# Attention and a two-layer block on one core: one fp32 identity, value scalings shared between two engines, and new orders for all engines

## The chip, the core and the metric

The kernel runs on one core of one Trainium2 chip. TensorE (PE in the profile) multiplies matrices; VectorE (DVE), ScalarE (ACT) and GpSimd (POOL) work on tiles; SyncE (SP) issues most transfers. The metric is the device time of one execution in microseconds. Durations are those of one profiled execution; lines of the program are written L692 for line 692.

## The reference, cut to what matters

Linear attention with a decay per head, in blocks of 64 positions, and then two dense layers with a "snake" between them. Batch 4, 8 heads, 768 positions, 64 values a head; 3072 rows of 512 go through layers of 2048 and 512.

```python
for b in range(nb):
    qb, kb, vb = (q[:, :, sl], k[:, :, sl], v[:, :, sl])
    intra = np.einsum('bhic,bhjc->bhij', qb, kb) * Dmask[None]
    intra = np.einsum('bhij,bhjd->bhid', intra, vb)
    inter = np.einsum('bhid,bhde->bhie', qb * lam_pow[None], kv_state)
    out[:, :, sl] = intra + inter
    kv_state = lam_block * kv_state + np.einsum('bhsd,bhse->bhde', kb * rev_pow[None], vb)
x = out.transpose(0, 2, 1, 3).reshape(B * S, H * D)
h = x @ w_in
s = np.sin(alpha * h)
g = h + s * s / (alpha + 1e-09)
return g @ w_out
```

`Dmask` is `lam ** (i - j)` for `i >= j` and 0 above the diagonal.

## The kernel before, in words

The work is cut into 24 units and 6 groups. A unit is four heads of one batch entry over 256 positions; four units make a group of 512 rows, which then goes through both layers. Each piece of work is an operation with a name, and u is its unit, g its group, f one of 16 column blocks of 128 of the first layer, m one of four row blocks:

- `ld{u}q`, `ld{u}k`, `ld{u}v` (SP, L475) load 256 KB each; three buffers for each of q, k and v. `cq`, `ck` (L493, L495) cast q and k to bf16; `sv` (L501) multiplies v by the table `R`, the reciprocal of the decay powers.
- `tq`, `tk` (PE, L511) transpose q and k against the identity `iden`, and `e0{u}`, `e1{u}` (L518, L520) copy the result out of PSUM: `e02` is unit 2's q, `e12` its k. From unit 9 on a transposing transfer `dt` (SP, L524) does this.
- `sc` (PE, L535) makes scores, `mm` (DVE, L543) masks them, `kv` (PE, L569) makes the products for the state, `kc` (ACT, L623, L579) copies them out, `bx`, `d0`, `d1` (L597, L611) and `n0`, `n1` (L635) multiply by decay tables on POOL or DVE, `in` and `io` (PE, L645, L658) make the output, and `oe` (DVE, L677) multiplies it by the table `ET` and writes it to `xt`. For units 8 to 23 `step{u}` holds the PE part of two units at once.
- `f1_g_f` (PE, L692) is the first layer, `sn` (ACT, L699) the sine, `sq` (ACT L706 or POOL L708) its square, `g_g_f` (DVE, L711) the sum, written to `gall`. `f1_0_0` is cut into two halves, `f1_0_0_0` and `f1_0_0_1`. `f2_g_m_j` (PE, L728) is a quarter of the second layer, four matmuls of 512 columns; `ev` (ACT, L734) copies the result out and `out` (SP, L759) sends it. The very last block, group 5 and m = 3, is cut by columns into 256, 128 and 128 (`f2_5_3_ja`, `b`, `c`) with `end0` to `end2` and `send0` to `send2`.
- `wi0` to `wi3` and `wo0` to `wo3` are the loads of the weights, issued by POOL (L457, L462): `wi0` brings columns 0 to 255 of `w_in`, `wi1` 256 to 767, `wi2` 768 to 1279, `wi3` the rest.
- `warm` (PE, L768) is filler, a matmul of ones of 512 or 256 columns.

At the start, two small inputs are loaded by ACT. `lamb` (PE, L405) spreads `lam` over the partitions, `tabc` (DVE, L408) copies it, `tab1` (POOL, L411) raises it to the powers of the position, `tabm` (DVE, L415) and `tab2` (DVE, L418) make the tables `E` and `R`, `tabi` (POOL, L422) makes two 64x64 identities in `id2`, `tabd` (POOL, L426 and L428) multiplies them by `E`, `tab0` (PE, L434) turns that into the evictions' table, `tab4` and `tab3` copy it to `LBD` and `ET`. `alpha` (PE, L446) transposes alpha against an identity `idf`, and `alphav` (DVE) copies it and takes its reciprocal.

What each engine does, in which order, is written out by hand in the table `SEQ` (L173): five lists of names. An engine takes its list from the front, strictly in order. A planner (`Plan.run`, L47) replays the lists with a cost per operation, only to settle in which order the program's instructions are written and which of several buffers each takes. PSUM has four banks `f` (first layer, second layer, transposes, early kv products, filler), one for scores (`s`) and a pair for outputs (`okv`); operations give a bank back when its last reader is done. The output buffers `ob` are three.

Of the kernel before, what the change touches and what calls it, by code (L numbers as in the profile page):

```python
# [12 lines left out]
FP32 = mybir.dt.float32  # L13
# [16 lines left out]
class Plan:  # L30
# [6 lines left out]
    HOLD, SHARE = 1.5, 0.35  # L37

# [8 lines left out]
    def run(self, seq):  # L47
# [28 lines left out]
        while len(order) < len(self.ops):  # L76
# [28 lines left out]
            for e in self.ENG:  # L105
# [9 lines left out]
                if e == "PE" and op.mode is not None:  # L115
                    c += self.SWITCH * (op.mode != mode)
                    mode = op.mode
                op.start, op.eng = t, e
# [3 lines left out]
                free[e] = t + c  # L122
# [23 lines left out]
def kernel(  # L146
# [28 lines left out]
            "warm warm warm warm lamb warm warm warm warm warm warm warm warm warm warm warm tq0 "  # L175
            "warm alpha tk0 warm warm warm tq1 warm tab0 kv0 sc0 tk1 warm tq2 warm warm warm sc1 "
# [29 lines left out]
        "DVE":  # L206
# [17 lines left out]
        "ACT":  # L224
# [65 lines left out]
    NXT = 3  # L290
    WI = (256, 512, 512, 768)
    WO = (4, 4, 4, 4)
    HALVES = ()
    NWARM = 9
    NLAM = 2
    DMAT = {9, 10, 11, 12, 13, 14, 15, 16, 17, 18, 19, 20, 21, 22, 23}
# [782 lines left out]
```

## Time and profile before

| | |
|---|---|
| time, median of 3 runs | 215.76 us (215.47 to 215.77) |
| the profiled execution | 215.8 us, its span 214.0 us |
| granted TensorE clock over the span | 1.000 |
| DVE busy | 119.7 us, 56% of the span |
| ACT busy | 138.9 us, 65% |
| POOL busy | 131.4 us, 61% |
| chain that ended last: PE's share | 91% |
| bytes moved | 33.65 MB, mean 157 GB/s |

The span runs from the first to the last instruction; the device time is 1.8 us longer in this execution. Busy shares are means over stages that differ: PE fills with filler and small products at the start and with large matmuls later, POOL has its work in the first 140 us, and DVE and ACT are thin in the last 50 us.

```profile
PE   8988999999999999999999999999999999999993
DVE  2387775557388774676968868865546224212101
ACT  3573788555699667878888789466578746336021
POOL 7998899297899699898988998530351030002100
DMA  5999999989899999899977744031240022031544
```

These are tenths of busy time in 40 slices of 5.35 us each.

### The profile page before, as it was taken

Reading aid. Unit: us, or ns where it says so; the run is one execution under the profiler, and the core shown is the slowest. Engines: PE = TensorE matmul, PEld = TensorE weight load, DVE = VectorE, ACT = ScalarE, POOL = GpSimd, SP = SyncE. Lnnn points to the kernel's source line nnn. Section 1 sums busy time; section 2 is a strip of 40 time slices with the busy share of each in tenths; the row PEclk is TensorE's granted clock in tenths of the full one; section 3 lists DMA queues with packets and bytes.
Section 4 is the critical chain, followed back from the end, with each engine's and each line's share of the span. In section 5 each row is a group of like instructions: output and inputs, shape, how many; then the busy total and the mean of one; then the engine's idle time right before and its main releaser. Section 6 shows DMA issues by size and latency. Waiting matters only on the chain.

```text
span 214.0 us, 5247 instructions
## 1 busy us (share of the span) xinstructions
PE 205.2 (96%) x2053; PEld 106.5 (50%) x2082; DVE 119.7 (56%) x175; ACT 138.9 (65%) x251; POOL 131.4 (61%) x212
## 2 busy tenths in 40 slices
PE   8988999999999999999999999999999999999993
PEld 3656444455445555555555555554444444444543
DVE  2387775557388774676968868865546224212101
ACT  3573788555699667878888789466578746336021
POOL 7998899297899699898988998530351030002100
PEclk9999999999999999999999999999999999999999
DMA  5999999989899999899977744031240022031544
GB/s 162 303 284 205 204 162 173 283 233 287 248 247 294 229 200 253 265 241 216 293 177 188 164 91 84 3 72 29 49 98 2 0 52 49 0 73 42 135 91 107
DMA packets 62347, 33.65 MB, mean 157 GB/s; under 512 B 18018, under 2 KB 59378, under 8 KB 62322
## 3 DMA queue, kind: packets, MB, share of 16 engines
q1 hardware_dynamic: 57824, 28.91, 57.4%
q0 software_dynamic: 4224, 4.19, 12.5%
q8 instruction: 16, 0.26, 0.5%
q10 hardware_dynamic: 274, 0.21, 0.3%
q14 instruction: 9, 0.07, 0.1%
HBM read 27.27 MB, written 6.29 MB: 157 GB/s over the span
## 4 chain that ended last, share of the span: by engine, by line
PE 91%; DVE 2%; ACT 2%; POOL 2%; issue 1%
PE hps L692 38%; PE ops L728 36%; PE sp L535 3%; PE okv L728 3%; PE okv L658 3%; PE bz L768 3%; PE okv L645 2%; PE pt L511 1%; DVE gall L711 1%; PE okv L569 1%; POOL vb L501 1%; ACT s L699 1%; ACT s L706 1%; DVE sm L543 1%; PE kp L569 0%
## 5 line engine op out<-in xcount | busy, mean ns | idle before, releaser
L711 DVE SCALAR_TENSOR_TENSOR gall<-s,r_sb,hps 128x512 bf16<-128x512 bf16 (+1 forms) x97 | 69.6, 739 | 59.7 <-ACT s L706 42.6
L692 PE MATMUL hps<-xt,w_in_sb 128*128 128x512 bf16 (+1 forms) x367 | 90.3, 377 | 1.7 <-DVE gall L711 0.4
L699 ACT ACTIVATE s<-hps,alpha_sb 128x512 bf16<-128x512 f32 (+1 forms) x97 | 65.5, 680 | 28.5 <-PE hps L692 27.4
L728 PE MATMUL ops<-w_out_sb,gall 128*128 128x512 bf16 (+2 forms) x378 | 82.1, 361 | 0.6 <-issue 0.5
L708 POOL TENSOR_TENSOR s<-s 128x512 bf16<-128x512 bf16 x31 | 32.2, 1042 | 48.6 <-ACT s L699 46.5
L728 PEld LDWEIGHTS <-gall 128*128 128x128 bf16 x416 | 38.8, 98 | 41.9 <-DVE gall L711 0.2
L692 PEld LDWEIGHTS <-w_in_sb 128*128 128x128 bf16 x388 | 36.4, 98 | 42.0 <-issue 1.7
L706 ACT ACTIVATE s<-s 128x512 bf16<-128x512 bf16 (+1 forms) x66 | 40.3, 621 | 1.2
L543 DVE TENSOR_TENSOR sm<-sp,mask 128x1024 bf16<-128x1024 f32 x24 | 29.2, 1218 | 1.2 <-PE sp L535 1.2
L501 POOL TENSOR_TENSOR vb<-st_v,R 128x512 bf16<-128x512 f32 x24 | 25.0, 1044 | 1.4 <-DMA st_v<-in_v_dram 0.9
L734 ACT COPY ob<-ops 128x512 f32<-128x512 f32 x21 | 12.2, 585 | 18.8 <-PE ops L728 18.8
L597 POOL TENSOR_TENSOR kvbd<-kvx,LBD 128x256 bf16<-128x256 f32 x32 | 19.7, 614 | 2.5
L677 DVE TENSOR_TENSOR xt<-okv,ET 128x512 bf16<-128x512 f32 x24 | 16.5, 687 | 6.2 <-ACT kva L579 3.9
L594 POOL TENSOR_TENSOR kvx<-kva,kvs 128x128 f32<-128x128 f32 x32 | 14.6, 456 | 6.9 <-ACT kva L579 6.7
L495 POOL CAST qk<-st_k 128x512 bf16<-128x512 f32 x18 | 10.9, 614 | 4.1 <-DMA st_k<-in_k_dram 4.1
L535 PE MATMUL sp<-qt 64*64 64x128 bf16 x384 | 10.2, 221 | 0.8 <-issue 0.4
L493 ACT CAST qk<-st_q 128x512 bf16<-128x512 f32 x13 | 8.0, 622 | 3.8 <-DMA st_q<-in_q_dram 3.8
L658 PE MATMUL okv<-sm,vb 64*64 64x128 bf16 x384 | 9.7, 218 | 0.5 <-DVE sm L543 0.5
L768 PE MATMUL bz<-const-bfloat16-1.0 128*128 128x256 bf16 (+1 forms) x33 | 9.2, 395 | 0.8 <-PEq L1063 0.8
L518 ACT COPY qt<-pt 128x512 bf16<-128x512 bf16 x11 | 6.4, 591 | 5.2 <-PE pt L511 5.2
L579 ACT COPY kva<-okv 128x256 f32<-128x256 f32 (+1 forms) x16 | 5.1, 316 | 6.9 <-PE okv L569 6.8
L635 POOL TENSOR_TENSOR kvs<-kvx,ET 128x128 f32<-128x128 f32 x24 | 9.4, 403 | 0.0
(63 smaller groups left out, 109.9 us busy)
## 6 DMA issues: line engine op xcount, KB each, us to landing
st_q<-in_q_dram SPq DMA_DIRECT2D x24, 256.0 KB, 4.6
st_k<-in_k_dram SPq DMA_DIRECT2D x23, 256.0 KB, 4.3
out_dram<-ob SPq DMA_DIRECT2D x45, 128.0 KB, 2.4
st_v<-in_v_dram SPq DMA_DIRECT2D x22, 256.0 KB, 4.5
w_out_sb<-in_moe_w_out_dram POOLq DMA_DIRECT2D x4, 512.0 KB, 8.7
w_in_sb<-in_moe_w_in_dram POOLq DMA_DIRECT2D x2, 512.0 KB, 7.3
w_in_sb<-in_moe_w_in_dram POOLq DMA_DIRECT2D x1, 768.0 KB, 10.3
st_v<-in_v_dram SPq DMA_DIRECT2D x4, 128.0 KB, 3.5
```

What stands on the lines that cost most here:

```text
L501: ENGINE[op.eng].tensor_tensor(out=T[u, "vb"][:], in0=T[u, "v"][:].rearrange("p h two e -> p two h e"), in1=R[:, :, hs].unsqueeze(3).to_br ...
L535: nc.tensor.matmul(out=T[u, "sp"][half[c], hd, par, hp, :], lhsT=QT[half[hd], 1, par, hp, half[c]], rhs=QT[half[hd], 0, :, hp, half[c]], s ...
L543: V.tensor_tensor(out=T[u, "sm"][:].rearrange("p hd par hp i -> p (hd par) hp i"), in0=T[u, "sp"][:].rearrange("p hd par hp i -> p (hd par ...
L597: G.tensor_tensor(out=bd[:], in0=X.unsqueeze(2).to_broadcast([P, 2, 2, D]), in1=LBD[:, hs, :].unsqueeze(3).to_broadcast([P, 2, 2, D]), op= ...
L658: nc.tensor.matmul(out=okv[half[hd], c, hp * P:(hp + 1) * P], lhsT=VB[half[c], par, 2 * hp + hd, :], rhs=ST[half[c], hd, par, hp, :], star ...
L677: V.tensor_tensor(out=o, in0=i, in1=ET[:, 2 * hh:2 * hh + 2].rearrange("p hp two e -> p hp (two e)") .unsqueeze(1).to_broadcast([P, 2, 2, ...
L692: op.ins = nc.tensor.matmul(out=op.tile[:, cols], lhsT=w_in_sb[:, c, f * P:(f + 1) * P], rhs=xt[g][:, c].rearrange("p b c i -> p (b c i)") ...
L699: A.activation(out=op.tile[:, cols], in_=mm.tile[:, cols], func=ACTF.Sin, scale=alpha_sb[:, f:f + 1])
L706: A.activation(out=op.tile[:, cols], in_=s1, func=ACTF.Square)
L708: ENGINE[op.eng].tensor_tensor(out=op.tile[:, cols], in0=s1, in1=s1, op=ALU.mult)
L711: V.scalar_tensor_tensor(out=gall[g][:, f, cols], in0=sq.tile[:, cols], scalar=r_sb[:, f:f + 1], in1=mm.tile[:, cols], op0=ALU.mult, op1=A ...
L728: op.ins = nc.tensor.matmul(out=first.tile[:, cols], lhsT=gall[g][:, f, m * P:(m + 1) * P], rhs=w_out_sb[:, f, cols], start=(f == 0), stop ...
```

## The change

A single fp32 identity of 128x128 is made on POOL; DVE copies from it the bf16 identity and the two 64x64 ones; `tabi` is gone, `tabd` and 14 of the 24 `sv` go to DVE, and one query cast goes from ACT to DVE. All five lists in `SEQ` are new; the number of fillers (33) stays. The planner gets two corrections to its costs and `out_5_0` another cost. Where each operation runs, counted from the lists:

| | before | after |
|---|---|---|
| `sv` | POOL 24 | POOL 10, DVE 14 (units 0, 2, 4, 6, 8, 11, 13 to 16, 19 to 22) |
| `cq`, `ck` | ACT 18, POOL 29, DVE 1 | ACT 15, POOL 32, DVE 1 |
| `e0`, `e1` | ACT 11, DVE 7 | ACT 10, DVE 8 |
| `sq` | ACT 66, POOL 31 | ACT 64, POOL 33 |
| `warm` ahead of `f1_0_0_0` | 33 | 26 |

```diff
-    iden = consts.tile([P, P], BF16, name="iden")
-    make_identity(nc, iden[:])
-    idf = consts.tile([NFC, NFC], FP32, name="idf")
-    make_identity(nc, idf[:])
+    idf = consts.tile([P, P], FP32, name="idf")
+    make_identity(nc, idf[:])
+    iden = consts.tile([P, P], BF16, name="iden")
     id2 = consts.tile([P, D], FP32, name="id2")
...
+    for c in range(2):
+        V.tensor_copy(out=id2[half[c], :], in_=idf[half[c], half[c]])
+    V.tensor_copy(out=iden[:], in_=idf[:])
...
-    def tables_i(op):
-        for c in range(2):
-            make_identity(nc, id2[half[c], :])
-
     def tables_d(op):
+        eng = ENGINE[op.eng]
         for hd in range(2):
-            G.tensor_copy(out=E2[half[hd]], in_=E[half[hd]]
+            eng.tensor_copy(out=E2[half[hd]], in_=E[half[hd]]
...
-        G.tensor_tensor(out=ED[:], in0=id2[:].unsqueeze(1).to_broadcast([P, HP * 2, D]),
+        eng.tensor_tensor(out=ED[:], in0=id2[:].unsqueeze(1).to_broadcast([P, HP * 2, D]),
...
-    SV = [("POOL", 1.05)]
+    SV = [("POOL", 1.05), ("DVE", .83)]
...
+    COLD = 6.9
+    OVER = {"PE": 0, "DVE": .08, "ACT": .09, "POOL": .04, "SP": 0}
...
+                    c *= 2 if t < self.COLD else 1
...
-                free[e] = t + c
+                free[e] = t + max(c - self.OVER[e], .02)
```

The lists, up to the first full block of the first layer and around the places that are spoken of:

```diff
 "PE":
-  warm warm warm warm lamb warm x11 tq0 warm alpha tk0 warm x3 tq1 warm tab0 kv0 sc0 tk1 warm tq2
-  warm x3 sc1 warm tk2 kv1 in0 io0 sc2 warm kv2 warm in1 tq3 io1 warm tk3 in2 io2 sc3 kv3 warm x2
-  tq4 in3 warm x3 io3 f1_0_0_0 tk4 f1_0_0_1 f1_0_1 sc4 kv4 f1_0_5 in4 f1_0_2 ...
+  warm x5 lamb warm x5 alpha tq1 tq0 warm tk0 tab0 warm x2 sc0 tk1 kv0 warm tq2 warm sc1 in0 tk2
+  warm kv2 io0 sc2 kv1 warm x6 tq3 warm tk3 in1 io1 tq4 sc3 warm kv3 warm x2 in2 io2 tk4 in3 io3
+  f1_0_0_0 kv4 sc4 f1_0_1 f1_0_0_1 f1_0_4 f1_0_5 in4 io4 f1_0_3 f1_0_2 warm f1_0_7 warm f1_0_8
+  warm f1_0_6 ... tq5 f2_0_0_3 tq6 tk5 f2_0_3_2 sc5 kv6 tk6 f2_0_3_3 kv5 sc6 warm tq7 ...
+  f1_1_9 warm warm f1_1_0 ... f2_5_3_2a f2_5_3_3a warm f2_5_3_0b ...
 "DVE":
-  tabc tabm tab2 ck0 alphav tab4 mm0 e02 mm1 oe0 mm2 oe1 e13 oe2 bx3 mm3 oe3 e14 ...
+  tabc tabm tabd cq0 tab2 e10 e00 sv0 tab4 alphav mm0 sv2 mm1 oe0 mm2 e13 oe1 mm3 bx3 oe2 e14 sv4 oe3
+  bx4 mm4 ... sv6 e15 e06 mm5 ... oe7 e08 sv8 e18 ... g_1_14 sv15 oe11 sv14 sv13 mm12 ...
 "ACT":
-  cq0 e00 cq1 e01 e10 kc0 tab3 e11 ck2 e12 kc1 cq3 kc2 ck3 e03 cq4 e04 kc3 ...
+  cq1 e01 ck1 e11 kc0 tab3 ck2 e12 e02 kc2 kc1 ck3 cq4 e03 ck4 e04 kc3 ...
 "POOL":
-  iden tab1 tabi tabd sv0 ck1 cq2 bx0 sv1 wi0 sv2 bx1 wi1 bx2 sv3 wi2 wi3 ck4 n03 ...
+  iden tab1 ck0 cq2 bx0 sv1 wi0 cq3 wi1 bx1 sv3 bx2 wi2 wi3 n02 wo0 ...
 "SP":
-  ld0k ld0q ld1q ld0v ld1k ld2q ld1v ld2k ld2v ld3q ld3v ld3k ld4q ld4k ld4v ... out_5_2 send0 out_5_1
-  out_5_0 send1 send2
+  ld1q ld0q ld0k ld1k ld0v ld2q ld2k ld2v ld1v ld3q ld4q ld3k ld3v ld4k ld4v ... out_4_1 out_5_0 send0
+  send1 send2
```

More of the change, by code (lines that the diff above doesn't have):

```diff
@@ L174 @@
         "PE":
-            "warm warm warm warm lamb warm warm warm warm warm warm warm warm warm warm warm tq0 "
-            "warm alpha tk0 warm warm warm tq1 warm tab0 kv0 sc0 tk1 warm tq2 warm warm warm sc1 "
[29 rows of a table removed]
-        "DVE":
[17 rows of a table removed]
-        "ACT":
[30 rows of a table removed]
-        "POOL":
[21 rows of a table removed]
+            "warm warm warm warm warm lamb warm warm warm warm warm alpha tq1 tq0 warm tk0 tab0 warm "
[31 rows of a table added]
+        "DVE":
[18 rows of a table added]
+        "ACT":
[28 rows of a table added]
+        "POOL":
[20 rows of a table added]
     }
     QS = set()
-    CK0 = [("ACT", .62), ("DVE", .43)]
     SPLIT = {(22, 2), (23, 1), (23, 2)}
@@ L292 @@
     WO = (4, 4, 4, 4)
-    HALVES = ()
+    HALVES = ({0}, set())
     NWARM = 9
@@ L296 @@
     DMAT = {9, 10, 11, 12, 13, 14, 15, 16, 17, 18, 19, 20, 21, 22, 23}
-    NH0 = 1
     KVF = {0, 1, 2, 3, 4, 5}
@@ L304 @@
     CK = [("ACT", .62), ("POOL", .62)]
-    SV = [("POOL", 1.05)]
-    EV0 = [('DVE', 0.41), ('ACT', 0.59)]
-    EV1 = [('DVE', 0.41), ('ACT', 0.59)]
+    SV = [("POOL", 1.05), ("DVE", .83)]
+    EVH = [("DVE", 0.42), ("ACT", 0.59)]
+    CK0 = [("ACT", .62), ("POOL", .62), ("DVE", .43)]
     dw = lambda cols: {128: .030, 256: .05, 384: .066, 512: .081, 640: .1, 768: .12, 1024: .16}[cols]
@@ L445, in alphas @@
         ap = bank(op, "f", [P, NFC], FP32, "ap")
-        nc.tensor.transpose(out=ap[:], in_=alpha_r[:], identity=idf[:])
+        nc.tensor.transpose(out=ap[:], in_=alpha_r[:], identity=idf[:NFC, :NFC])
         op.tile = ap
@@ L770, in dummy @@
                              start=True, stop=True)
-        dop = add("warm", on("PE", 0.40), [], dummy, take=("f",), mode="n")
+        dop = add("warm", on("PE", 0.2135), [], dummy, take=("f",), mode="n")
         dop.give, dop.part = ((dop, "f"),), 1
@@ L775 @@
     idq = add("iden", on("POOL", 1.85), [], lambda op: None)
-    lamd = add("lamb", on("PE", .4), [lamq, first], lam_all, take=("f",), lag=PEL, mode="n")
+    lamd = add("lamb", on("PE", .1), [lamq, first], lam_all, take=("f",), lag=PEL, mode="n")
     tbc = add("tabc", on("DVE", .12), [lamd], tables_c, give=((lamd, "f"),))
@@ L779 @@
     tbm = add("tabm", on("DVE", .17), [tb1], tables_m)
-    tbi = add("tabi", on("POOL", .95), [idq], tables_i)
-    tbd = add("tabd", on("POOL", 1.7), [tbm, tbi], tables_d)
+    tbd = add("tabd", [("POOL", 1.55), ("DVE", .95)], [tbm, idq], tables_d)
     tb2 = add("tab2", on("DVE", .25), [tbm], tables_v)
@@ L787 @@
     alq = add("alq", on("ACT", .01), [lamq], lambda op: None, lag=1.2)
-    alphas_op = add("alpha", on("PE", 0.2), [alq], alphas, take=("f",), lag=PEL, mode="n")
+    alphas_op = add("alpha", on("PE", 0.16), [alq, idq], alphas, take=("f",), lag=PEL, mode="n")
     al2 = add("alphav", on("DVE", 0.4), [alphas_op], alphas_v, give=((alphas_op, "f"),))
@@ L813, in make_unit @@
         early = u < NT
-        cq = add(f"cq{u}", CQS if u in QS else CQ if u else CK0, [lq, tbm if u in QS else None],
+        cq = add(f"cq{u}", CQS if u in QS else CK if u else CK0, [lq, tbm if u in QS else None],
                  lambda op: cast(op, u, 0), take=("qk",), give=((lq, "st0"),),
@@ L821, in make_unit @@
         if u not in DMAT:
-            tq = add(f"tq{u}", on("PE", .22), [cq], lambda op: turn_pe(op, u, 0),
+            tq = add(f"tq{u}", on("PE", .22), [cq, idq], lambda op: turn_pe(op, u, 0),
                      take=("f", "qt"), give=((cq, "qk"),), lag=PEL, mode="n")
-            e0 = add(f"e0{u}", EV0, [tq], lambda op: turn_ev(op, tq, u, 0),
+            e0 = add(f"e0{u}", EVH, [tq], lambda op: turn_ev(op, tq, u, 0),
                      give=((tq, "f"),))
@@ L827, in make_unit @@
                      take=("f",), give=((cq, "qk"),), lag=PEL, mode="n")
-            e1 = add(f"e1{u}", EV1, [tk], lambda op: turn_ev(op, tk, u, 1),
+            e1 = add(f"e1{u}", EVH, [tk], lambda op: turn_ev(op, tk, u, 1),
                      give=((tk, "f"),))
@@ L994, in make_f2 @@
                  take=("ob",), give=owe)
-        st = add(f"out_{g}_{m}", on("SP", 1.0), [ev], lambda op: f2st(op, ev, g, m),
+        st = add(f"out_{g}_{m}", on("SP", .55 if (g, m) == (NG - 1, 0) else 1.0), [ev], lambda op: f2st(op, ev, g, m),
                  give=((ev, "ob"),), dma=(.65, .08))
@@ L1017 @@
     assert at == {"i": DFF, "o": NFC}
-    for f in range(NFC):
-        for hb in ((0, 1) if f < NH0 else (None,)):
-            make_f1(0, f, hb)
-    for hb in ((0, 1) if 1 in HALVES else (None,)):
+    for g in range(2):
         for f in range(NFC):
-            make_f1(1, f, hb)
+            for hb in ((0, 1) if f in HALVES[g] else (None,)):
+                make_f1(g, f, hb)
     def gate_of(x):
```

192 rows, old and new, of the table SEQ are left out of this document.

## The prediction, made before the changed kernel was run

> **What bounds the kernel now.** I read the table by stage first. Its columns are the stretch, its length, busy time and instruction count of PE, PEld, DVE, ACT and POOL, then granted clock, DMA share and GB/s.
>
> ```profile
> 15.00:20.00 5.00, 3.69 (x101) 2.73 (x99) 3.41 (x6) 2.14 (x6) 4.28 (x8) 1.00 1.28 214
> 22.69:54.42 31.73, 31.22 (x307) 15.55 (x312) 20.46 (x29) 21.05 (x41) 25.01 (x38) 1.00 1.06 228
> 60.00:140.00 80.00, 79.03 (x1003) 42.26 (x1020) 59.24 (x78) 63.70 (x114) 69.45 (x116) 1.00 0.87 193
> 150.00:205.00 55.00, 54.74 (x260) 25.67 (x264) 17.86 (x25) 28.73 (x48) 10.37 (x10) 1.00 0.22 49
> ```
>
> Behind 22.69 us TensorE stands still for 0.5, 1.0 and 0.3 us in the three later rows, and much of that is missing matmul records: a run of n matmuls of 512 columns goes at 0.216 us each (24 in 5.18 us in the chain of waits), and where the count of a run is one short the gap is 0.22. So past 22.69 nothing but TensorE's own work sets the time, and no order can win there; it can only lose. What is not TensorE's work lies ahead of it. The timeline of PE at the start (start, duration, line, tiles, count, idle time before with what ended it):
>
> ```profile
> 0.77 1.87 PE L768 MATMUL bz<-const-bfloat16-1.0 128*128 128x512 bf16 x4 [0.77 <-PEq L1063]
> 2.56 0.59 PE L405 MATMUL lp<-lam_r,row 1*128 1x8 f32 x2
> 3.09 3.55 PE L768 MATMUL bz<-const-bfloat16-1.0 128*128 128x512 bf16 x11
> 7.30 0.49 PE L768 MATMUL bz<-const-bfloat16-1.0 128*128 128x256 bf16 x3
> 19.74 0.61 PE L692 MATMUL hps<-xt,w_in_sb 128*128 128x256 bf16 x4
> 22.69 1.02 PE L692 MATMUL hps<-xt,w_in_sb 128*128 128x512 bf16 x4 [0.18 <-DVE gall L711]
> ```
>
> L768 is filler, which costs nothing as long as TensorE would wait. All 33 fillers lie ahead of 18.9 us. At 22.69 units 0 to 3, unit 4 up to its scores and kv product, and f1_0_0_0, f1_0_0_1 and f1_0_1 are done. That point compares the two orders. Before it a chain over DVE, ACT and POOL counts, and the weights:
>
> ```profile
> 6.84 1.04 POOL L428 TENSOR_TENSOR ED<-id,E 128x512 f32<-128x512 f32 x1
> 7.84 1.04 POOL L501 TENSOR_TENSOR vb<-st_v,R 128x512 bf16<-128x512 f32 x1
> 11.79 0.95 POOL L457 DMA_DIRECT2D w_in_sb<-in_moe_w_in_dram  x1
> 14.34 0.80 POOL L457 DMA_DIRECT2D w_in_sb<-in_moe_w_in_dram  x1
> 10.08 1.23 DVE L543 TENSOR_TENSOR sm<-sp,mask 128x1024 bf16<-128x1024 f32 x1 [0.29 <-PE sp L535]
> 18.12 1.22 DVE L543 TENSOR_TENSOR sm<-sp,mask 128x1024 bf16<-128x1024 f32 x1
> w_in_sb<-in_moe_w_in_dram POOLq DMA_DIRECT2D x2, 512.0 KB, 7.3
> ```
>
> **Identities.** POOL loses the 16x16 pair (0.10 + 0.19) and L422's four instructions with their gaps (5.09 to 6.34, 1.25 us). DVE gains three copies, by its nearest row (the copy at L408, 0.17) 0.5 us, between 2.41 and 3.19 where it waits for lp. They cost nothing; without that cover, up to 0.5 on the chain.
>
> **The start, step by step** (before's time in brackets). PE now runs five fillers ahead of lamb, 0.427 each (1.87 us hold four): lamb 2.92 (2.56). With before's own distances lam_bc 3.55, the power on POOL 3.80 to 5.48, E complete 5.7. tabd on DVE: two copies at 0.17 and a product whose nearest row is the mask at L388 (0.69, two f32 inputs in SBUF; above, POOL's 1.04): done 6.75 (7.88). cq0 moves from ACT to DVE behind it, 0.36: 7.05, so tq0 at 7.1 (6.47), tk0 7.45, tab0 7.7 (8.40), sc0 8.85 (9.61). Ahead of the first mask DVE has e10 and e00 (0.41 each), sv0 (0.69 to 1.04; I take 0.69, from the row of the same engine and size), tab4 0.33, alphav 0.42: first mask 9.9 (10.08). Second, behind sv2: 11.66 (11.83). Third: sc2 waits for e02, queued on ACT behind kc0, tab3, ck2 and e12 from 10.1 (0.43, 0.60, 0.65, 0.59, then 0.59): 13.7 (13.77). Fourth: sv1's v is now the ninth load; before's ninth was issued at 6.26, and st_v takes 4.5 to 5.4, so about 11.65; then on POOL sv1 1.04, the first w_in issue 0.95, cq3 0.61, the second issue 0.80, bx1 0.61: 15.6. in1 and io1 follow at 15.85, oe1 16.3, sc3 16.45, mask 16.94 (18.12). Then bx3 0.42, oe2 to 19.1 (okv has one buffer: in3 waits for it), io3 19.35, f1_0_0_0 19.7 (19.74), kv4 and sc4 to 20.75, oe3 20.7, f1_0_1 20.75 and f1_0_0_1 (0.86 + 0.43): f1_0_4 at 22.1 with the same work done as before at 22.69. **Lead 0.59 us.** Bounds: none, if the three scalings on DVE take 1.04 and ACT's queue is as tight as worked out; and 1.1, because f1_0_4 reads columns of the second w_in transfer, which before lands at 14.34 + 7.2 = 21.6. The same 15 loads and the first w_in transfer lie ahead of it, and the DMA share is full from 5 us on, so no order of POOL brings it earlier.
>
> **Fillers.** Of the same 33 seven now stand behind 22 us: after f1_0_2, f1_0_7 and f1_0_8, one after sc6, two after f1_1_9, one ahead of the last end block. Each is 0.11 (three start within 0.22 us). Where before has no waits, a filler is lost time, and where after has one there, that wait is the loss: +0.76; bounds 0.33 (the three around units 5 to 8 hidden by those units' latency, and one more) and 0.77.
>
> **Units 5 to 7** hang on loads gated by the second w_out transfer. Seven second-layer blocks instead of eight lie between tq5 and the last io; one block of 0.86 stands ahead of tq5 instead. sv6 on DVE ahead of e15 waits for its v, now fourth in that row of loads instead of sixth. ck5 and cq5 waited for loads (4.13 and 0.89 us idle), so this chain gives nothing; I cost it 0, its cover being the seven blocks (6.0 us), and half a block, 0.4, if one wait shows.
>
> **Ten more scalings on DVE** (14 in all) in the stage of steps: 10 x 0.69 = 6.9, DVE 66.1 of 80 us busy instead of 59.2; POOL 10.4 less. Queued behind each are masks, oe and gates, for which PE's banks wait. Between two steps stand about four blocks of 0.86, which cover one scaling, or two ahead of mask 12 (1.4). I take +0.1, bounds 0 and 1.6 (0.1 a step). Three casts and two squares fewer on ACT (3 x 0.62 + 2 x 0.62 = 3.1 us) meet an engine with waits of 27 us for hps: 0.
>
> **Loads and transposes** on SP keep their number; each is moved past others, but their waits end on casts, and PE stood behind none of them: 0. The planner's COLD and OVER are no instructions.
>
> **Tail.** The last two column blocks are 0.89 apart as before. ev_5_0 ends 2.1 us ahead of the last matmul, out_5_0 goes out on SP (0.47) and ACT (0.55), and end0, on ACT behind that issue, starts 0.3 late; send0 (0.59 twice) then pushes send1 and send2 on SP, the last starting 0.58 after the last matmul instead of 0.34 (ACT's 0.39): +0.1, bounds -0.3 (out_5_0's 256 KB are out of the way) and +0.4.
>
> Sum: -0.59 + 0.76 + 0.10 + 0.10 = +0.37. The profiled execution is 215.8 (span 214.0 and 1.8 around it), the median 215.76: **216.1 us**.
>
> [...] DVE L388 ran from 1.69 to 2.38; POOL's select of a 128x128 tile began at 1.89 and took 0.65, against 0.23 to 0.24 for 64x64: it ended 0.16 after L388. [...]
>
> **Rivals.** (1) *The lead reaches the weights.* ACT's and POOL's queues run looser than worked out, f1_0_4 starts at 21.6, and the three middle fillers vanish in waits of units 5 to 8: -1.1 + 0.43 + 0.1, 215.2. For it: the fourth mask gains 1.2 us. Against: e02 and sv1 stand behind four others. It decides from f1_0_4 before 21.75.
>
> [...]
>
> (3) *The clock opens late.* Fillers of 512 columns go at 0.43 us until 5.2, 128 columns at 0.056 from 6.47: half pace, then full. After leaves PE empty from 6.0 to 7.1. At half pace tab0 takes 1.9 instead of 0.96 and the first mask comes 0.45 later: 216.5. [...]
>
> (4) *The start wins nothing*: lead 0, 216.7.
>
> **Numbers.** Within 0.2% (0.43 us) is what a measurement here cannot tell from no change. Forecast 0.45, own range 215.7 to 216.7, about half on each side of 216.19: same 0.22, slower 0.23. Rival 1 0.22: faster 0.15, same 0.07. Rival 2 0.23, rivals 3 and 4 0.05 each: slower. Together faster 0.15, same 0.29, slower 0.56; range 215.1 to 217.6.
>
> **What would show it.** lp at 2.9; first mask 9.9, fourth near 16.9; f1_0_4 near 22.1; filler rows after 22 us with no wait ahead of them; PE idle in 60 to 140 within 0.3 of before's; the last SP issue 0.6 after the last matmul. Wrong would be a start of f1_0_4 ahead of 21.5, or a wait of a us or more on PE behind sm, xt or gall.

## The result and the profile after

The changed kernel takes 221.26 us (220.62 to 222.06), the kernel before, on the same chip, 215.64 us (215.47 to 215.90): a ratio of 1.026, 95% interval 1.024 to 1.029. It is slower by 5.6 us, and far outside of the range forecast. Three kernels further down (x3_cq0act, x4_ld13v, f1_pool) had one slow execution each, more than 1.5% above their fastest; medians and ratios leave it out.

The profiled execution has a span of 219.4 us against 214.0. Three distances add up to it: f1_0_0_0 starts at 22.09 us instead of 19.74 (+2.35), from there to the last matmul it takes 193.13 us instead of 190.69 (+2.44), and from the last matmul to the end of the span 4.19 instead of 3.59 (+0.60). Here and below the last matmul is placed where its weight load ends, 0.04 to 0.05 us behind its start.

The busy tenths of the changed kernel in 40 slices of its span:

```profile
PE   8788999999999999799999999999999999999992
DVE  3688766528568974989959995986645552100001
ACT  3266788637389663797896778679657883311120
POOL 6259765499789989997867796433353001100000
DMA  6999999997999999998979756002021131242163
```

TensorE looks as full as before, but for the 7 in the second slice (5.5 to 11.0 us) and the 7 in the 17th (87.8 to 93.2 us), of which more below. A full PE row does not mean useful work: fillers, products at half pace and lost turns count as busy. Here is the table by stage (stretch, length, busy time and count of PE, PEld, DVE, ACT, POOL, then granted clock, DMA share, GB/s):

```profile
15.00:20.00 5.00, 4.42 (x136) 3.28 (x124) 4.05 (x6) 4.34 (x12) 4.98 (x8) 1.00 0.86 136
22.69:54.42 31.73, 31.15 (x312) 15.37 (x312) 19.54 (x31) 22.76 (x44) 22.83 (x38) 1.00 1.08 222
60.00:140.00 80.00, 78.36 (x960) 41.02 (x958) 65.12 (x85) 61.96 (x112) 66.95 (x107) 1.00 0.90 201
150.00:205.00 55.00, 55.00 (x275) 25.33 (x274) 18.80 (x26) 29.31 (x48) 10.17 (x10) 1.00 0.21 49
```

In the stage of steps DVE rose from 59.2 to 65.1 us, near the 66.1 worked out. POOL fell by 2.5 only, from 69.45 to 66.95, though its scalings in this stretch went from 14 to 6 (14.6 us to 6.3): two squares and two casts more came in, and a cast took 0.68 us in the mean instead of 0.61.

**The start.** The timeline of PE (start, duration, line, tiles, count, idle time before with what ended it):

```profile
0.78 2.29 PE L767 MATMUL bz<-const-bfloat16-1.0 128*128 128x512 bf16 x5 [0.78 <-PEq L1059]
3.00 0.59 PE L407 MATMUL lp<-lam_r,row 1*128 1x8 f32 x2
5.77 0.61 PE L510 MATMUL pt<-iden,qk 128*128 128x128 bf16 x4
7.64 0.61 PE L510 MATMUL pt<-iden,qk 128*128 128x128 bf16 x4 [1.27 <-DVE qk L494]
8.69 2.02 PE L433 MATMUL et<-ED,ones 128*128 128x512 f32 x2
11.06 0.64 PE L534 MATMUL sp<-qt 64*64 64x128 bf16 x16
```

lp comes at 3.00 as forecast (2.92). Then tq0 (7.64) waits for cq0 on DVE, and PE is empty for 1.27 us. The trace's record of the clock has it open at 12.73 us, where before it opened at 6.45. Until then the rows show half pace: fillers of 512 columns at 0.42 us each (five in 2.10) instead of 0.22, four transposes in 0.61 us instead of 0.40, tab0 in 2.02 instead of the 0.96 worked out. The first mask starts at 11.76 us instead of 9.9.

**The fillers behind 22 us.**

```profile
28.44 0.27 PE L767 MATMUL bz<-const-bfloat16-1.0 128*128 128x256 bf16 x1
28.77 1.02 PE L691 MATMUL hps<-xt,w_in_sb 128*128 128x512 bf16 x4
29.63 0.27 PE L767 MATMUL bz<-const-bfloat16-1.0 128*128 128x256 bf16 x1
29.96 1.02 PE L691 MATMUL hps<-xt,w_in_sb 128*128 128x512 bf16 x4
```

A block of four goes on after 0.86 us (28.77 to 29.63), but the block behind a filler starts 0.33 us after the filler did. The filler's own turn is 0.11; the other 0.22 is a wait for the filler's end. The trace has it: the block at 29.96 waits for one semaphore, the one that the filler ahead of it raises as it ends, at 29.90. That fits a block that takes over the filler's bank. The last filler, at 213.33, has a follower without such a wait, and it costs 0.11. The seven together take 1.87 us in these rows.

**Step 13.** DVE, then SP, then PE:

```profile
84.78 1.11 DVE L500 TENSOR_TENSOR vb<-st_v,R 128x512 bf16<-128x512 f32 x1
88.27 0.89 DVE L500 TENSOR_TENSOR vb<-st_v,R 128x512 bf16<-128x512 f32 x1 [2.38 <-POOL s L707]
89.08 1.21 DVE L542 TENSOR_TENSOR sm<-sp,mask 128x1024 bf16<-128x1024 f32 x1
```

```profile
81.20 2.54 SPq L758 DMA_DIRECT2D out_dram<-ob  x4
83.84 0.53 SPq L474 DMA_DIRECT2D st_v<-in_v_dram  x1
```

```profile
88.83 0.39 PE L644 MATMUL okv<-qt,kvbd 128*128 128x128 bf16 x4
90.34 0.42 PE L534 MATMUL sp<-qt 64*64 64x128 bf16 x16 [1.12 <-DVE sm L542]
```

The scaling at 88.27 is sv13. It waits 2.38 us, the mask of unit 12 stands behind it, and PE waits 1.12 us for the mask: the 7 in the row of tenths. The trace names a square on POOL as the releaser, but sv13 needs its v: ld13v stands on SP behind the four transfers of out_0_1 and out_0_2 and is issued at 83.84 only.

**The tail.** SP's last transfers, after and then before:

```profile
213.31 3.84 SPq L748 DMA_DIRECT2D out_dram<-ob  x5
```

```profile
209.50 1.92 SPq L749 DMA_DIRECT2D out_dram<-ob  x3
```

Five transfers in a row instead of three; the last issue starts 1.22 us behind the last matmul, where before none starts later than 0.58 (on ACT).

### The profile page after: what moved, and what is told of

Same layout as the page of the kernel before. It is cut to its first block, busy times and chain, and to the rows that moved or that the text cites. A ratio compares the mean times of both kernels' runs of the same rounds, so it can differ in the third digit from the quotient of the medians.

```text
span 219.4 us, 5283 instructions
## 1 busy us (share of the span) xinstructions
PE 209.5 (95%) x2082; PEld 107.2 (49%) x2082; DVE 131.7 (60%) x196; ACT 134.8 (61%) x245; POOL 121.7 (55%) x194
## 3 DMA queue, kind: packets, MB, share of 16 engines
q0 software_dynamic: 4224, 4.19, 12.1%
## 4 chain that ended last, share of the span: by engine, by line
PE 71%; POOL 13%; ACT 4%; DVE 4%; issue 3%; DMA 3%; POOLq 0%; ACTq 0%
PE ops L727 30%; PE hps L691 28%; PE okv L727 3%; POOL qk L494 3%; DMA qt<-qk 3%; POOL s L707 3%; PE sp L534 3%; ACT s L698 2%; POOL vb L500 2%; POOL kvbd L596 2%; PE okv L657 2%; POOL kvs L634 2%; PE bz L767 1%; PE okv L644 1%; PE pt L510 1%
## 5 line engine op out<-in xcount | busy, mean ns | idle before, releaser
L691 PE MATMUL hps<-xt,w_in_sb 128*128 128x512 bf16 (+1 forms) x388 | 91.4, 377 | 0.6 <-DVE gall L710 0.4
L727 PE MATMUL ops<-w_out_sb,gall 128*128 128x512 bf16 (+2 forms) x384 | 83.3, 361 | 0.0
L707 POOL TENSOR_TENSOR s<-s 128x512 bf16<-128x512 bf16 (+1 forms) x33 | 33.8, 1027 | 48.2 <-ACT s L698 42.3
L705 ACT ACTIVATE s<-s 128x512 bf16<-128x512 bf16 x64 | 39.1, 627 | 1.0
L593 POOL TENSOR_TENSOR kvx<-kva,kvs 128x128 f32<-128x128 f32 x32 | 15.5, 483 | 6.2 <-ACT kva L578 6.0
L494 POOL CAST qk<-st_k 128x512 bf16<-128x512 f32 x19 | 12.5, 662 | 2.9 <-PE hps L691 2.3
L500 DVE TENSOR_TENSOR vb<-st_v,R 128x512 bf16<-128x512 f32 x14 | 11.6, 832 | 4.0 <-POOL s L707 2.4
L634 POOL TENSOR_TENSOR kvs<-kvx,ET 128x128 f32<-128x128 f32 x24 | 11.1, 462 | 0.0
L500 POOL TENSOR_TENSOR vb<-st_v,R 128x512 bf16<-128x512 f32 x10 | 10.4, 1043 | 0.0
L494 POOL CAST qk<-st_q 128x512 bf16<-128x512 f32 x13 | 8.4, 653 | 2.9 <-DMA st_q<-in_q_dram 2.9
```

What stands on the lines that cost most here:

```text
L494: ENGINE[op.eng].tensor_copy(out=o, in_=i)
L500: ENGINE[op.eng].tensor_tensor(out=T[u, "vb"][:], in0=T[u, "v"][:].rearrange("p h two e -> p two h e"), in1=R[:, :, hs].unsqueeze(3).to_br ...
L691: op.ins = nc.tensor.matmul(out=op.tile[:, cols], lhsT=w_in_sb[:, c, f * P:(f + 1) * P], rhs=xt[g][:, c].rearrange("p b c i -> p (b c i)") ...
L705: A.activation(out=op.tile[:, cols], in_=s1, func=ACTF.Square)
L707: ENGINE[op.eng].tensor_tensor(out=op.tile[:, cols], in0=s1, in1=s1, op=ALU.mult)
L727: op.ins = nc.tensor.matmul(out=first.tile[:, cols], lhsT=gall[g][:, f, m * P:(m + 1) * P], rhs=w_out_sb[:, f, cols], start=(f == 0), stop ...
```

## The experiments

All times are medians; ratios are to the kernel before on the same chip, with 95% intervals. The median of the kernel before lay between 215.25 and 215.64 us on these chips, so a difference between two medians below can be off by some 0.4 us. The diffs are in the lists of the program's table.

| kernel | us | ratio | f1_0_0_0 | to the last matmul | clock opens |
|---|---|---|---|---|---|
| before, as first profiled | 215.76 | 1 | 19.74 | 190.69 | 6.45 |
| after | 221.26 | 1.026 (1.024 to 1.029) | 22.09 | 193.13 | 12.73 |
| x1_fill | 219.44 | 1.018 (1.013 to 1.023) | 20.38 | 193.19 | 7.14 |
| x3_cq0act | 218.50 | 1.013 (1.009 to 1.017) | 19.78 | 192.23 | 5.41 |
| x2_nolate | 218.91 | 1.016 (1.012 to 1.020) | 21.64 | 191.02 | 4.64, closed 8.05 to 11.46 |
| x4_ld13v | 219.69 | 1.020 (1.014 to 1.026) | 21.55 | 192.15 | 5.13, closed 8.54 to 11.96 |
| c1_three | 218.27 | 1.012 (1.007 to 1.016) | 20.59 | 192.42 | 6.86 |
| c2_tail | 216.95 | 1.006 (1.003 to 1.008) | 21.36 | 190.69 | 9.65 |
| d1_best | 216.35 | 1.005 (1.003 to 1.007) | 21.24 | 190.77 | 4.92, closed 8.33 to 11.74 |
| e1_hole | 217.11 | 1.008 (1.006 to 1.011) | 20.16 | 191.68 | 4.93 |
| f1_pool | 221.45 | 1.027 (1.022 to 1.032) | 20.21 | 195.61 | 4.59 |
| y1_hole | 215.84 | 1.001 (0.999 to 1.003) | 19.14 | 191.34 | 4.53 |
| y2_latefill | 216.05 | 1.003 (1.001 to 1.005) | 19.05 | 191.46 | 4.24 |
| d2_ident | 215.58 | 1.001 (0.999 to 1.003) | 18.54 | 190.56 | 4.33 |
| d3_scal | 216.38 | 1.005 (1.003 to 1.006) | 19.04 | 193.02 | 4.31 |
| f2_tail | 216.50 | 1.004 (1.002 to 1.006) | 19.21 | 190.92 | 4.78 |

The last three columns are of the one profiled execution of each kernel, whose time can lie a microsecond from the median; they tell where it goes, and the ratio how much it is. The first kernels, x and c, are the changed kernel with something put right; d1, e1 and f1 go on from there; y1, y2, d2, d3 and f2 are the kernel before with one piece of the change.

**x1_fill** closes the hole between tq1 and tq0 with filler.

```diff
 "PE":
-  alpha tq1 tq0
+  alpha tq1 warm warm warm warm warm warm tq0
```

> The changed kernel with six more 256-column fillers between tq1 and tq0, where TensorE stood empty for 1.27 us. Theory 1 (the hole keeps the clock at half pace until 12.7 us): the clock opens by about 6.5 to 9.5 us, f1_0_0_0 starts 1.5 to 2.3 us earlier than 22.1, the time falls from 221.3 to 219.0 to 220.0 us. Rival (the start is late because lamb, the tables and cq0 are queued late on DVE, whatever the clock): f1_0_0_0 within 0.3 us of 22.1, time 221.0 to 221.6.

219.44 us, 1.8 less. The clock opened at 7.14, the first mask at 10.43, and f1_0_0_0 started 1.71 us earlier. From there on nothing changed (193.19 against 193.13).

**x3_cq0act** takes the wait away instead: the cast goes back to ACT.

```diff
 "ACT":
-  cq1 e01
+  cq1 cq0 e01
 "DVE":
-  tabd cq0 tab2
+  tabd tab2
```

> The changed kernel with unit 0's query cast back on ACT. Theory 1 (cq0 behind tabd on DVE makes the hole, the hole makes the clock late): tq0 follows tq1 without a hole, the clock is open by 9 us at the latest and does not close again, f1_0_0_0 at 20.0 to 20.8 us, 219.0 to 219.8 us. Rival (filler was needed for its own sake, a cast elsewhere does not matter): 221 or more.

218.50 us, 2.8 less, with f1_0_0_0 at 19.78, which is 2.31 us earlier than in the changed kernel. In x1_fill tq0 still waits for cq0, and TensorE is only kept busy meanwhile; that alone gave 1.71. So by these two executions the larger part of the loss at the start is the clock, and the rest the late cast. A hole remains (0.98 us ahead of tk0, which waits for a cast on POOL), and in this execution the clock stayed open through it.

**y1_hole** makes a hole in the kernel before.

```diff
 "PE":
-  lamb warm x11 tq0
+  lamb warm x5 tq0
```

> The kernel before without the six 256-column fillers ahead of tq0, so that TensorE is empty for about a microsecond near 6 to 8 us. Theory 1: the clock opens at 9 us or later instead of 6.45, the first masks come 0.5 to 1.5 us later, time 216.2 to 217.5 instead of 215.65. Rival (fillers at the start are worth nothing): 215.4 to 215.9, clock open by 6.5 us.

No change: 215.84 us. The clock opened at 4.53 and stayed open with holes of up to 0.41 us. The record of the clock changes 3.41 us apart in d1_best (4.92, 8.33, 11.74), and stretches of that length, laid from where it opened, show when it closed again in these executions. First y1_hole, then d1_best with two stretches, then e1_hole (columns as in the table by stage):

```profile
4.53:7.94 3.41, 2.38 (x22) 1.16 (x19) 1.13 (x5) 2.24 (x4) 3.05 (x9) 1.00 1.05 302
```

```profile
4.92:8.33 3.41, 1.72 (x18) 1.13 (x17) 1.40 (x6) 1.17 (x3) 0.81 (x2) 1.00 1.08 293
8.33:11.74 3.41, 3.41 (x40) 1.40 (x40) 2.96 (x8) 0.64 (x2) 0.61 (x1) 0.50 1.08 294
```

```profile
4.93:8.34 3.41, 3.18 (x26) 1.82 (x23) 2.11 (x7) 1.58 (x3) 0.81 (x2) 1.00 1.07 297
```

In y1_hole PE was busy 2.38 of 3.41 us, and the next stretch stayed at full pace. In d1_best it was busy 1.72, and the next one was granted 0.50; that one was full, and the clock was back at 11.74. In x2_nolate (1.52 busy) and x4_ld13v (1.74) it closed as well, in f1_pool (2.06) and x3_cq0act (2.43) not.

**x2_nolate** drops the seven late fillers.

```diff
 "PE":
-  f1_0_2 warm f1_0_7 warm f1_0_8 warm f1_0_6 ... sc6 warm tq7 ... f1_1_9 warm warm f1_1_0 ... f2_5_3_3a warm f2_5_3_0b
+  f1_0_2 f1_0_7 f1_0_8 f1_0_6 ... sc6 tq7 ... f1_1_9 f1_1_0 ... f2_5_3_3a f2_5_3_0b
```

> The changed kernel without its seven fillers behind 22 us. Theory 2 (a matmul that takes the bank of the filler just ahead of it waits for the filler's end, so that such a filler costs 0.33 us and not 0.11): 1.9 us less, 219.4 us. Rival A (0.11 each, as predicted): 0.8 us less, 220.5. Rival B (each fills a wait that is there anyway): 221.3 within 0.3.

218.91 us, 2.35 less. In the profiles f1_0_0_0 starts 0.45 us earlier, though nothing ahead of it was edited (the clock opened at another time), and from there to the last matmul it takes 2.11 less. Divided by seven that would be 0.3 a filler, near the 0.33 of the theory, but half of it is not the fillers' own. At the masks the lead over the changed kernel grows from 0.45 us (unit 4) to 1.47 (unit 11): 1.0 us for six fillers, so some 0.7 of the 1.76 us that they take in the rows stood where PE would have waited anyway. At unit 13 the lead is 2.5, because PE's wait of 1.12 us ahead of step 13 is gone as well, with ld13v still behind the two sends:

```profile
87.44 0.39 PE L643 MATMUL okv<-qt,kvbd 128*128 128x128 bf16 x4
87.86 0.42 PE L533 MATMUL sp<-qt 64*64 64x128 bf16 x16
```

Here ld13v is issued at 81.56 and sv13 waits for it 1.04 us (the trace names the load) instead of 2.38. The seventh filler is the last 0.1.

**y2_latefill** puts three fillers into the kernel before.

```diff
 "PE":
-  f1_0_2 f1_0_3 f1_0_4 io4 f1_0_8 f1_0_6
+  f1_0_2 warm f1_0_3 warm f1_0_4 io4 f1_0_8 warm f1_0_6
```

> The kernel before with three more 256-column fillers in the first layer's first group, each followed by a block of the first layer that takes the filler's bank. Theory 2 (0.33 us each): 215.3 + 1.0 = 216.3. Rival A (0.11 each): 215.6. Rival B (they fall into waits): 215.3 within 0.15.

216.05 us, +0.6 (interval +0.2 to +1.0): less than the 1.0 that three times 0.33 make. Against y1_hole, which reached the first layer at the same time, the mask of unit 5 starts 0.8 late (45.71 against 44.90), and that of unit 13 at the same time (90.07 and 90.03). Something of the loss is taken up in between.

**x4_ld13v** puts the load of unit 13's v ahead of the two sends.

```diff
 "SP":
-  ld15q out_0_1 out_0_2 ld13v dt13
+  ld15q ld13v out_0_1 out_0_2 dt13
```

> The changed kernel with the load of unit 13's v issued ahead of out_0_1 and out_0_2 on SP. Theory 3 (sv13 on DVE waits for this load at 88 us with mask 12 queued behind it, and TensorE waits 1.1 us for the mask): the wait ahead of step13 is gone, 1.1 to 1.3 us less, about 220.1. Rival (the step is late for its transposes or POOL's state chain, and DVE was only the last of several): less than 0.4 us gained, 220.9 or more.

219.69 us, 1.6 less; with three executions its interval reaches up to the changed kernel's. By the profiles 0.54 of it is an earlier start, which the edit does not touch, and 0.98 lies between f1_0_0_0 and the last matmul, a little under theory 3's 1.1. The mask of unit 12 starts at 85.52 instead of 89.08, and PE waits for no mask:

```profile
87.96 0.39 PE L644 MATMUL okv<-qt,kvbd 128*128 128x128 bf16 x4
88.27 0.42 PE L534 MATMUL sp<-qt 64*64 64x128 bf16 x16
```

So the load was the releaser, and not the square on POOL that the trace of the changed kernel names; in x2_nolate and x3_cq0act the trace names the load for the same wait of sv13.

**c1_three** joins x1_fill, x2_nolate and x4_ld13v.

> The changed kernel with all three edits: the hole at tq0 filled, no filler behind 22 us, the load of unit 13's v ahead of out_0_1 and out_0_2. Theory (three separate losses of 1.8, 2.35 and 1.25 us, which add): 221.3 - 5.4 = 215.9 us, within 0.5. Rival (they overlap, the slack of one is the wait of another, and a further loss in the steps is behind them): 217 us or more.

218.27 us: 3.0 less than the changed kernel, where the three alone make 4.8 (1.71 at the start, 2.11 and 0.98 behind it). They do not add up. About 1.0 is counted twice, because x2_nolate and x4_ld13v both take away the wait ahead of step 13. And in its profile PE waits 0.59 us ahead of step 18 for a transposing transfer, a wait that the changed kernel does not have there.

**c2_tail** is c1_three with another end.

```diff
 "PE":
-  f2_5_3_1a f2_5_0_2 f2_5_0_3 f2_5_3_2a f2_5_3_3a f2_5_3_0b
+  f2_5_3_1a f2_5_3_2a f2_5_3_3a f2_5_0_2 f2_5_0_3 f2_5_3_0b
 "ACT":
-  ev_4_1 ev_5_0 end0
+  ev_4_1 end0 ev_5_0
 "SP":
-  out_5_0 send0 send1
+  send0 out_5_0 send1
```

> The kernel with the three edits, and the first column block of the last piece finished before f2_5_0_2, so that send0 goes out ahead of out_5_0, as in the kernel before. Theory (after the last matmul SP still has four transfers to issue, at 0.5 to 0.85 us each, against two before, 0.64 us later at the end): 0.5 to 0.7 us less than the kernel with three edits, about 215.3. Rival (the end hangs on the landing of the last transfer, whenever it is issued): less than 0.2 us gained.

216.95 us, 1.3 less than c1_three, with wide intervals. More than the tail is in it: in its profile f1_0_0_0 starts 0.77 us later than in c1_three's, and from there to the last matmul it takes 1.73 less. The tail by itself is read from the profile: the last matmul to the end of the span takes 3.61 us, as before (3.59), instead of 4.19.

**f2_tail** gives the kernel before that end of after.

```diff
 "PE":
-  f2_5_3_0a f2_5_3_1a f2_5_2_1 f2_5_3_2a f2_5_3_3a f2_5_1_1 ... f2_5_0_2 f2_5_0_3 f2_5_3_0b
+  f2_5_3_0a f2_5_3_1a f2_5_2_1 f2_5_1_1 ... f2_5_0_2 f2_5_0_3 f2_5_3_2a f2_5_3_3a f2_5_3_0b
 "ACT":
-  ev_5_2 end0 ev_5_1 ev_5_0
+  ev_5_2 ev_5_1 ev_5_0 end0
 "SP":
-  send0 out_5_1 out_5_0 send1
+  out_5_1 out_5_0 send0 send1
```

> Before with after's tail alone: the last two parts of the first column block behind the last whole block, ev_5_0 ahead of end0 on ACT, out_5_0 ahead of send0 on SP. Theory (traces: the last issue starts 1.21 behind the last matmul in after, 0.57 in before): +0.6, 215.9 to 216.3. Rival (the prediction's +0.1): 215.4 to 215.8.

216.50 us, +0.9 (interval +0.5 to +1.3). The last matmul to the end of the span takes 4.19 us, the changed kernel's own figure. So the tail costs 0.6 by the profile and 0.5 to 1.3 by the times.

**d2_ident** is the changed program with the lists of before: tabi left out, tabd and all scalings on POOL.

```diff
 "POOL":
-  iden tab1 tabi tabd
+  iden tab1 tabd
```

> The program of after with the lists of before (tabi left out, tabd on POOL, all scalings on POOL): the single fp32 identity and DVE's three copies alone. Theory: the copies lie where DVE waits for lp, lam_bc at 3.2 as in before: 215.4 to 215.9, no change. Rival: the copies run longer than 0.17 each or wait for POOL, tabc comes 0.5 late and the start with it: 216.1.

215.58 us against 215.32: no change that can be measured. Its profiled execution took 214.47 us, the shortest shown here, with f1_0_0_0 at 18.54; its median does not bear a gain out.

**d3_scal** moves ten scalings in the kernel before from POOL to DVE.

```diff
 "POOL":
-  sv8 sv11 sv13 sv14 sv15 sv16 sv19 sv20 sv21 sv22
 "DVE":
-  e08 ... e18 ... oe11 mm12 ... oe12 g_2_14 ... oe13 g_2_8 ... oe14 ... mm18 g_3_14 ... mm20 g_3_4
+  e08 sv11 ... e18 sv8 ... oe11 sv16 mm12 sv13 ... oe12 sv14 g_2_14 sv15 ... oe13 g_2_8 sv19 ... oe14 sv21
+  ... mm18 g_3_14 sv20 ... mm20 g_3_4 sv22
```

> Before with ten scalings (units 8, 11, 13 to 16, 19 to 22) moved from POOL to DVE, all else as it was. Theory of the prediction: they cost 0.1, 215.7. Rival (the two engines take turns, a scaling is stretched from 0.69 to about 0.9 or more and stands ahead of masks and gates): 216.5 to 217.4, with new waits of PE on gall or sm of 0.3 us or more. Third: POOL, eased by 10 us, feeds the transposing transfers earlier, and the waits around step 13 shrink: 215.2.

216.38 us, +1.06 (interval +0.6 to +1.4). The rows show both engines longer at work where they meet. DVE and POOL of d3_scal:

```profile
82.00 1.13 DVE L500 TENSOR_TENSOR vb<-st_v,R 128x512 bf16<-128x512 f32 x1
83.05 1.21 DVE L542 TENSOR_TENSOR sm<-sp,mask 128x1024 bf16<-128x1024 f32 x1
```

```profile
81.97 0.61 POOL L596 TENSOR_TENSOR kvbd<-kvx,LBD 128x256 bf16<-128x256 f32 x1
82.53 1.07 POOL L494 CAST qk<-st_k 128x512 bf16<-128x512 f32 x1
```

The scaling starts 0.03 us behind a POOL instruction of 0.61 and takes 1.13 instead of 0.69 (the next one, at 84.19 with POOL idle, takes 0.68); the cast on POOL starts while it is under way and takes 1.07 instead of 0.61. So where the two met, both took longer, by 0.44 and 0.46 us; what held them up was not shown. The ten scalings took 0.89 us in the mean:

```profile
L500 DVE TENSOR_TENSOR vb<-st_v,R 128x512 bf16<-128x512 f32 x10 | 8.9, 889 | 0.0
```

What PE lost by it is less clear. In this execution, which took 217.45 us and so 1.07 more than the median, PE waits twice 0.3 us for gall and once 0.9 us, ahead of step 13, for a transposing transfer. That transfer was issued at 79.92, 1.3 us behind the end of the last cast ahead of it, and landed 6.5 us later, where before it took 5.0; between 83.5 and 85.0 the core's transfers moved only 5 to 10 GB/s. So the largest wait here is not one for DVE or POOL. The price is measured, the longer rows are seen, and that the one comes of the other is not shown.

**d1_best** joins the repairs: x2_nolate, x4_ld13v, c2_tail's end, x3_cq0act, and lamb behind four fillers instead of five.

> All repairs together: no late fillers, ld13v ahead of the two sends, last column block's first part earlier and end0 and send0 ahead of ev_5_0 and out_5_0, the cast cq0 back on ACT, and lamb after four fillers instead of five. Theory: from f1_0_0_0 to the last matmul c2_tail takes as long as before (212.05 - 21.36 and 210.43 - 19.74 are both 190.69 us), so all that is left of its loss is the late start. x3_cq0act started f1_0_0_0 at 19.78; with lamb 0.4 earlier 19.4 to 19.8. Then last matmul at 210.1 to 210.5 and the time 215.2 to 215.8, no different from before. Rival: the moved scalings and casts make waits in the steps as soon as the start is early (in y1_hole a start 0.6 earlier was swallowed there): 216.3 to 216.8.

216.35 us, +1.0: nearer to the rival. In its profiled execution the work from f1_0_0_0 on is level with before, and the start is late by 1.5, mostly because the clock closed again at 8.33 (the two stretches above; with the clock open, e1_hole below starts 1.08 earlier). That execution took 217.37 us, more than the median. Of the eleven it alone has a mean granted clock as low as 0.992; the other ten have 0.997 to 1.000 and a median of 216.3, so the clock that closed again is not what makes the +1.0.

**e1_hole** fills that hole, with five fillers more between tq0 and tk0 (its expectation says six).

```diff
 "PE":
-  tq1 tq0 warm tk0
+  tq1 tq0 warm x6 tk0
```

> d1_best and six fillers more, between tq0 and tk0, where d1_best leaves TensorE empty for 1.69 us (5.89 to 7.85; tk0 waits for the cast of unit 0's k, whose load is the third to land) and the clock fell to half from 8.33 to 11.74. Theory: what is left of d1_best's loss is the clock alone, since from f1_0_0_0 to its last matmul it takes 190.77 us and before 190.69. With the hole filled the clock stays open, f1_0_0_0 starts at 19.4 to 20.0, the last matmul at 210.2 to 210.8, and the time is 215.2 to 215.9, no different from before. Rival: the scalings on VectorE cost in the steps, as d3_scal had it (+1.06): 216.2 to 216.7 though the clock stays open.

217.11 us: the clock stayed open, f1_0_0_0 came 1.08 earlier than in d1_best's profile, and the time was no better (ratio 1.008 against 1.005). The theory falls, and the time lies above the rival's range too. In the profiles the masks of units 13 to 17 start 1.38 us ahead of d1_best's, that of unit 20 by 0.48, that of unit 22 by 0.16: the lead is lost between steps 17 and 22. Ahead of the scores of unit 20 PE shows a wait, and on POOL stands what it comes from (PE, then POOL):

```profile
125.58 0.34 PE L644 MATMUL okv<-qt,kvbd 128*128 128x128 bf16 x3 [0.46 <-POOL kvbd L596]
```

```profile
122.26 0.61 POOL L494 CAST qk<-st_k 128x512 bf16<-128x512 f32 x1 [0.87 <-DMA st_k<-in_k_dram]
```

POOL waits 0.87 us for a load before it can cast, and the decay product that PE needs is queued behind. Here an earlier start runs into a load that comes no earlier.

**f1_pool** takes the ten scalings in d1_best back to POOL.

```diff
 "DVE":
-  sv8 sv11 sv15 sv14 sv13 sv16 sv19 sv22 sv20 sv21
 "POOL":
-  sq_1_8 sv9 ... sv12 cq12 ... d111 ck17 d012 ... n08 d110 ... cq16 ... d112 ... d014 ... d115 ... n114
+  sq_1_8 sv8 sv9 ... sv12 sv11 cq12 ... d111 sv13 ck17 d012 sv14 ... n08 d110 sv15 ... cq16 sv16 ...
+  d112 sv19 ... sv22 d014 ... d115 sv20 ... n114 sv21
```

> d1_best with the ten scalings of the stage of steps back on POOL, near the same times. Theory: the last microsecond of d1_best is the scalings on VectorE (d3_scal: +1.06): 215.2 to 215.7. Rival: it is in the orders of loads and casts, whatever engine scales, and POOL then has 10.4 us more between 60 and 140: 216.3 to 217.5.

221.45 us, as slow as the changed kernel. POOL is busy for 70.3 of the 80 us of the steps, about as in the kernel before, yet PE waits 2.1 us in one place for it:

```profile
PE okv L645 <- POOL kvbd L597: 2.1, 1, 2.1
PE hps L692 <- DVE gall L711: 0.9, 2, 0.7
```

The places on POOL were chosen by hand and can be poor, so this does not give a price of the scalings; it shows that d1_best's last microsecond is not won back by this move alone.

## Why the prediction was wrong

The forecast was 216.1 us, in a range up to 217.6. What the profile before said of the kernel held: TensorE's own work fills the span behind 22 us, and the new orders could only lose there. The terms failed, nearly all on the same side. In the profiles the changed kernel reaches f1_0_4 1.71 us late, takes 3.08 longer from there to the last matmul and 0.60 longer behind it. In the 3.08 stand fillers of 1.87 us and waits of PE of 0.35 (gall), 0.46 (a transposing transfer ahead of step 12) and 1.12 (the mask ahead of step 13), where the kernel before waits 0.24. That is 0.5 more than the difference; what goes faster by so much was not traced.

**The start, forecast -0.59, was +1.71.** The same point, f1_0_4 with equal work behind it, is at 24.40 us (two blocks of 0.86 and 0.43 behind 23.11) and not at 22.1. The steps up to lp held. Then two steps failed. The wait of tq0 for cq0 was seen ("after leaves PE empty from 6.0 to 7.1") and taken as a gap; with it the clock also stayed at half pace until 12.73 (7.14 in x1_fill, where the gap is filled). That the clock opens late is rival 3. It was given a chance of 0.05 and 0.45 us, reckoned on tab0 alone, where everything up to the first mask ran at half pace and the mask came 1.86 us late. x1_fill (-1.8, with TensorE kept busy and tq0 no earlier than in the changed kernel) and x3_cq0act (-2.8) show it. The moved fillers were costed by what they add where they stand now, and not by what they had covered where they stood.

**Fillers, forecast +0.76, take 1.87 us in the rows, and leaving them out gave 1.1** (x2_nolate: 1.0 for six, 0.1 for the last; its other 1.0 is the wait ahead of step 13). The mechanism was right and the price wrong: 0.11 is the distance between three fillers in a row, and a block behind a filler starts 0.33 later. The upper bound of 0.77 took the same 0.11 for certain. That some of it falls into waits was foreseen.

**Loads and transposes, forecast 0, were about +1.0** (x4_ld13v; the wait itself is 1.12 us). "Their waits end on casts, and PE stood behind none of them" was read in the kernel before. In the changed one sv13 is on DVE, so ld13v's wait is DVE's, and the mask behind it is PE's: the wait of a microsecond behind sm that the forecast had named as a sign of being wrong. The two changes were costed apart, and the price lies in their meeting. It is a close meeting: in x2_nolate, with the same order on SP, the load goes out early enough and PE does not wait.

**Ten scalings, forecast +0.10 with bounds 0 and 1.6**, cost +1.06 in the orders of before (d3_scal). That the scalings would cost so much had been given a chance of 0.23, as rival 2. Longer rows are there (0.89 us in the mean of ten instead of 0.69, and 1.13 where one met POOL), but no run shows what makes them longer, and PE's largest wait in that profile is another one. In the changed orders they cannot be priced alone: c2_tail and d1_best, which keep them, go from f1_0_0_0 to the last matmul as fast as before in their profiled executions. How much the stretched rows cost in the changed kernel stays open.

**The tail, forecast +0.10 with bounds -0.3 and +0.4**, is +0.6 (f2_tail). The last SP issue was expected 0.58 behind the end of the last matmul (0.34 in the kernel before) and starts 1.05 behind it. end0 waits on ACT for out_5_0's issue, and behind send0's two transfers those of send1 and send2 start on SP 0.85 apart (the first 0.76 long), where 0.59 had been put in.

**Identities, forecast 0**, held (d2_ident). Units 5 to 7 and the fewer casts on ACT were not tried apart.

The repairs do not add up as the losses do. x2_nolate and x4_ld13v share the wait ahead of step 13, and c1_three and e1_hole have new waits in the steps, where time won early is lost again. Of the 5.6 us the repairs of d1_best give back 4.6. What the last 1.0 is stays open. It is not the clock that closed again (the ten other executions of d1_best, and e1_hole). The longer rows of DVE and POOL where they meet and the loads in the steps are two candidates, from d3_scal and from e1_hole's row, and neither is shown in d1_best. No kernel here is faster than the kernel before.

## What to carry to other kernels

Filler can be holding something up. Before it is moved, ask what the place that it leaves needs of it (here the clock, which opened at 12.73 us instead of 6.45), and price it in the new place with the block behind it, which may wait for its end (here 0.22 us of the 0.33). When an operation changes its engine, work out anew which transfer it waits for and who is queued behind it on the new engine; a transfer that nobody waited for on one engine can stop TensorE from another (here for 1.12 us). And do not count on a gain that lies ahead of a chain of loads: x1_fill kept its lead of 1.7 us from the start to the end, and in e1_hole a lead of 1.1 to 1.4 us was lost where a load in the middle came no earlier.

## What the runs showed of the hardware

- In x2_nolate and d1_best the changes of the clock on record lie 3.41 us apart (open at 4.64, closed at 8.05, open at 11.46; 4.92, 8.33, 11.74), and in the changed kernel 204.8 us, 60 such stretches, from 12.73 to 217.53. Where they lie differs from run to run: the first opening was between 4.24 (y2_latefill) and 12.73 us. At the start it closed after stretches with PE busy 1.52 (x2_nolate), 1.72 (d1_best) and 1.74 us (x4_ld13v), and not after 2.06 (f1_pool), 2.38 (y1_hole) and 2.43 (x3_cq0act). In the last stretch with matmuls, behind 200 us, it stayed open after 1.52 (c1_three), 1.63 (y2_latefill) and 1.80 us (x1_fill), and closed after 1.27 (the changed kernel) and 1.31 (y1_hole). So the busy time of the rows alone does not tell these cases apart.
- In two executions, of the changed kernel and of c2_tail, a stretch whose rows fill 3.41 us (2.50 to 5.91, 2.83 to 6.24) did not open the clock. Both hold lp (0.59 us in the changed kernel) and alpha (0.28). Stretches with lp alone (d2_ident, 0.92 to 4.33) or alpha alone (x1_fill, 3.73 to 7.14) did open it; whether the two together keep it shut was not tried.
- The column of the granted clock shows 1.00 ahead of the first change on record, even where fillers of 512 columns go at 0.43 us (before, 0.77 to 2.64 us): the pace must be read from the rows there.
- A square of POOL was named as the releaser of a wait of 2.38 us (in the changed kernel) that a load ended (x4_ld13v, where the load goes out earlier and the mask behind it starts 3.56 us earlier).
- The scaling on DVE (0.68 us beside an idle POOL) took 1.13, and a cast on POOL (0.61 otherwise) 1.07, where the two met (d3_scal, 82.00 to 83.60 us).
